# A three-stage fused kernel (retention, gated feed-forward, routed experts): a different order of work at the start of the expert stage and inside its phases

## The chip, the cores and the metric

The kernel runs on one core of a Trainium2 chip. The metric is the time of one execution on the device in microseconds (us), the median of several runs. A profile of one further execution comes with it. Engines: PE (TensorE), DVE (VectorE), ACT (ScalarE), POOL (GpSimd), and SP, which only issues DMAs here.

## The reference, cut to what matters

Three layers follow each other on 2304 tokens of 512 values.

1. Retention: `scores = q @ k.T / 8`, multiplied by a decay matrix per head, times `v` (4 batches, 8 heads, 576 positions, 64 values).
2. Feed-forward: `h = x @ w_in` (2048 columns), `g = h * tanh(softplus(h))`, `y = g @ w_out`.
3. Routed experts: eight experts with 288 places each. The pairs (token, expert) are taken in the order of falling logit; a token gets the first expert that still has a place. Then, for every expert,

```python
mask = assigned == e
h = np.maximum(x[mask] @ w1[e], 0.0)      # 512 -> 1024
out[mask] = h @ w2[e]                     # 1024 -> 512
```

## The kernel before, in words

Matrix products are made from two fp32r pieces per operand, hi and lo (`hi*hi + hi*lo + lo*hi`), so a logical product is three matmuls. Layers 1 and 2 take the first 517 us of the profile and are not touched. They leave the rows `y` in DRAM (`ydram`), the logits `L` in SBUF, and tiles for the search. All that follows is in `second_part`.

**Phases.** The experts are settled one after another: phase `ph` finds the expert that fills up next, its 288 tokens, and computes it. The search (`routing_fast`, a generator) has three levels: DVE compares every token's best logit with 66 thresholds (`reach`, L719, in two instructions, tokens 0 to 8 and 9 to 17 of a partition), PE counts (`cnt`, L1003, 18 small matmuls), DVE picks the interval. A tail of short DVE instructions settles the expert (`EINT`), updates `L` and prepares the next search. The compaction (L878 to L932) turns token positions into a list of row numbers: DVE writes three one-hot tiles `hot` (L900), PE sums them into `pi` (L907, three times six small matmuls), DVE makes the integers `ix`. The `gather` (L1239) then fetches the rows by three indirect DMAs of 96 rows that POOL issues; `transposes` turns them on PE and splits them (ACT hi, DVE lo).

**The expert.** `ffn(ph)` issues 192 matmuls of 288 columns, yielding after each: eight column blocks of `w1` (12 matmuls each; L1287, output `hp`), then four of `w2` (24 each; L1301, output `op`). After each `hp` group ACT writes hi and DVE lo (`htl`, L1278); a later group's bank waits for them.

**Weights.** An expert has eight tiles of 128x1024 (512 KB). `fetch` issues the load on SP into one of four buffers `wraw`; `split` lets ACT write the hi tile and POOL the lo tile (L841, L843). Tile `i` of the first four holds row block `i` of `w1`, so any column block needs all four; the second four hold two row blocks of `w2` each, and again any output block needs all four.

**The order** is written out while the program is built. A set of estimated clocks (`clk`) follows each engine; after every expert matmul the loop decides by them whether to issue a search step, a piece of the compaction (`fills`), a due lo part (`urgent`), a split, a gather or a transpose. A search step ends where the generator yields its DVE cost and a PE cost. `pieces(ph, n)` forces splits until `n` tiles of a phase are made, on DVE for every second one: eight at matmul 92, four of the next phase at a phase's end.

**The start of the stage.** No expert work exists yet, so search 0, its compaction, the first gather, the split of the first four weight tiles (ACT hi, DVE lo), the first level of search 1 and the transposes follow in a fixed order (L1363 to L1387). All small PSUM values of the search, and `pi`, lie in one bank, `dv`; wherever PE writes a bank that DVE reads, the framework orders the two.

Of the kernel before, what the change touches and what calls it, by code (L numbers as in the profile page):

```python
# [7 lines left out]
F32 = mybir.dt.float32  # L8
# [619 lines left out]
DG = 0.05  # L628
RM = (0, 0.1)
X = mybir.AxisListType.X  # L630

# [142 lines left out]
def second_part(ctx, tc, L, ydram, wx, cst, out, st, fast, L0=None):  # L774
# [30 lines left out]
    else:  # L805
        off, one18 = st.off, st.one18
    spacer = c2.tile([1, 1], F32, name="spacer")

    def rt(shape, name, dt=F32, bufs=2):
# [8 lines left out]

    def fetch():

        while len(fetched) < 4 and SRC.get("next", 0) // 8 in EINT:
            n = SRC.get("next", 0)
            ph, i = n // 8, n % 8
            if i == 0:
                r = nc.sync.value_load(EINT[ph], min_val=0, max_val=E - 1)
                SRC[ph] = wx[bass.ds(r, 1)].rearrange("o p f -> p (o f)")
            raw = wk.tile([P, 1024], F32, tag="wraw", name="wraw", bufs=4)
            if n == 4:

# [47 lines left out]
    def compaction(ph, slot):  # L877


        if fast:  # L880
            pi = pi_[ph % 2][:96].rearrange("p (k c) -> p k c", c=2)
            col, col1, at = col_[ph % 2], col1_[ph % 2], at_[ph % 2]
        else:
            pi = psum.tile([96, 3, 2], F32, tag="pi", name="pi")
            col = col1 = rt([P, NT], "col")
            at = rt([P, NT], "at", BF)
# [11 lines left out]
        def part(c0, ready, n=6):  # L898
            hot = rt([P, n, 96], "hot", BF, bufs=3)
            V.tensor_tensor(hot, bc(io[:, None, :], [P, n, 96]),  # L900
                            bc(at[:, c0:c0 + n, None], [P, n, 96]), op=ALU.is_equal)
            on_dve(0.75)
            ready[:] = [clk["dve"] + 0.15]
            yield
            clk["pe"] += 0.06 * n
            for c in range(n):
                nc.tensor.matmul(pi, hot[:, c, :], cv[:, c0 + c, :, :], start=(c0 + c == 0),  # L907
                                 stop=(c0 + c == NT - 1))
# [17 lines left out]
        fills.append((None, go(gens[1][1])))  # L926
        fills.append((gens[0][0], go(gens[0][1])))
        fills.append((None, go(gens[2][1])))
        fills.append((gens[1][0], go(gens[1][1])))
        fills.append((gens[2][0], go(gens[2][1])))  # L930
        fills.append((None, end))
        COMP.append(ph)  # L932

    def routing_fast():
# [29 lines left out]
        for ph in range(E):  # L964
            sel = rt([P, NT], "sel")
            rs = rt([P, 1], "rs", BF)
            if ph < E - 1:
# [7 lines left out]
                for lv in range(3):  # L975
                    end = lv == 2
                    if lv or ph:
                        ind = st.tile([P, NT, NW], "ind", BF)
                        st.reach(ind, tau, NW, 0, 9)
                        if not lv:  # L980
                            st.one_hot(0, NT)
                        st.reach(ind, tau, NW, 9, NT)
# [4 lines left out]
                    if end:  # L987
                        below = rt([P, 1], "below")
                        V.tensor_scalar(below, tau[:, 0:1], stp[:, 2:3], None, op0=ALU.subtract)
                    yield (F0[ph > 0], F1, F2)[lv], 0.65  # L990
                    if not (ph or lv):
# [40 lines left out]
                m0 = rt([P, NT], "m0n")  # L1032
                V.tensor_reduce(m0, L, axis=X, op=ALU.max)
                its = rt([P, NT], "its")
                V.tensor_tensor(its, m, m0, op=ALU.is_gt)
# [16 lines left out]
            EINT[ph] = ei[0:1, 0:1]  # L1052
            pend = (ph, sel, rs, dm)
            if ph < 2 or ph >= E - 2:
                yield 2.4, 0.06
                rest, pend = slots(*pend), None
                rest()
                yield 1.2, 0.0
# [178 lines left out]
    scat = []  # L1237

    def gather(ph):  # L1239
        xg = wk.tile([96, 3, DM], F32, tag="xg", name="xg")  # L1240
        for k in range(3):
            nc.gpsimd.indirect_dma_start(
                out=xg[:, k, :], out_offset=None, in_=ydram[:, :],
                in_offset=bass.IndirectOffsetOnAxis(ap=IDX[ph][:, k:k + 1], axis=0))
        XG[ph] = xg

# [22 lines left out]
    def ffn(ph):  # L1269
# [11 lines left out]
        for ft in range(F // P):  # L1281
            hp = psum.tile([P, CAP], F32, tag="fp", name="hp", bufs=3)
            s = slice(ft * P, (ft + 1) * P)
            k = 0
            for w, x in ((0, xh), (0, xl), (1, xh)):
                for kt in range(KT):
                    nc.tensor.matmul(hp, W[kt][w][:, s], x[:, kt, :], start=(k == 0), stop=(k == 11))  # L1287
                    k += 1
                    if k == 12:
                        nc.scalar.activation(hh[:, ft, :], hp, AF.Relu)  # L1290
                        urgent.append((clk["pe"] + (0.6 if ft < F // P - 1 else 0.0), lambda ft=ft, hp=hp: rest(ft, hp)))
                    yield
        ot = wk.tile([P, KT, CAP], F32, tag="ot", name="ot")
        OT[ph] = ot
        for dt in range(KT):
            op = psum.tile([P, CAP], F32, tag="fp", name="op", bufs=3)
            k = 0
            for w, h in ((0, hh), (1, hh), (0, hl)):
                for ft in range(F // P):
                    s = slice((ft % 2) * DM + dt * P, (ft % 2) * DM + (dt + 1) * P)  # L1300
                    nc.tensor.matmul(op, W[4 + ft // 2][w][:, s], h[:, ft, :], start=(k == 0),  # L1301
                                     stop=(k == 23))
# [45 lines left out]
    def step():  # L1348

        clk["pe"] = max(clk["pe"], clk["route"]) + nxt_pe[0]  # L1350
        try:
            cost, nxt_pe[0] = next(gen)
            on_dve(cost, clk["pe"] + 0.25)
            clk["route"] = clk["dve"] + 0.15
        except StopIteration:
            clk["route"] = 1e9

    def pieces(ph, n):
        while len(WSET.get(ph, ())) < n:
            fetch()  # L1360
            split(eng=V if len(WSET.get(ph, ())) % 2 else None)

    while 0 not in EINT:  # L1363
        step()
    fetch()
    los = [split(True) for i in range(4)]
# [17 lines left out]
    rush(True)  # L1384
    clk["pe"] = max(clk["pe"], clk["dve"])
    step()
    fetch()  # L1387
    for ph in range(E):
# [9 lines left out]
        for i, _ in enumerate(ffn(ph)):  # L1398
# [22 lines left out]
            if i in todo:  # L1421
# [5 lines left out]
        if nxt:  # L1427
# [12 lines left out]
            rush(True)  # L1440
            pieces(ph + 1, 4)
    while fills:
# [62 lines left out]
def host_layout(inputs):  # L1505
# [18 lines left out]
        "wx": c(np.concatenate([  # L1524
            inputs["moe2_w1"].reshape(E, KT, P, F).transpose(0, 2, 1, 3).reshape(E, P, KT * F),
            inputs["moe2_w2"].reshape(E, F // P, P, DM).transpose(0, 2, 1, 3).reshape(E, P, F // P * DM)], 2)),
    }
# [44 lines left out]
```

## Time and profile before

| | |
|---|---|
| three timed runs | 812.0, 812.57, 812.8 us; median 812.57 |
| profiled execution | 811.79 us, of which span 810.0 us |
| busy in the span | PE 758.4 us, POOL 475.3, DVE 543.7, ACT 435.7 |
| layers 1 and 2 | 0 to 517 us |
| start of the expert stage | 517 to 544 us |
| eight phases | 544 to 797 us |
| last stores | 797 to 810 us |

Times in the trace are counted from the start of the span. A matmul's end is modelled: a lone one shows 0.29 us where the next one starts 0.13 us later, so PE can look busy over a short loss; a loss is read from starts.

### The profile page before, as it was taken

The numbers are of one execution on the slowest core, as the hardware profiler recorded it, in microseconds if no ns is written. First come the engines' busy times: TensorE is split into PE (matmuls) and PEld (weight loads), VectorE is DVE, ScalarE is ACT, GpSimd is POOL, SyncE is SP. The second block draws the span as 40 slices with busy tenths as digits, with TensorE's granted clock in tenths as the row PEclk, the third lists the DMA queues.
The fourth block names the chain that finished last, engine by engine and source line by source line (L and its number), as shares of the span: only waits on it lengthen the run. The fifth ranks groups of instructions, "written<-read, shape, count | busy, mean of one in ns | idle before, by whom it ended". The sixth has DMA issues, their size and how long they took to land.

```text
span 810.0 us, 16286 instructions
## 1 busy us (share of the span) xinstructions
PE 758.4 (94%) x6163; PEld 699.2 (86%) x6163; DVE 543.7 (67%) x1262; ACT 435.7 (54%) x943; POOL 475.3 (59%) x539
## 2 busy tenths in 40 slices
PE   7799899999999999999999999849999999999993
PEld 6687777898988898999889899739999999999992
DVE  5999998645556898997989955676567473442110
ACT  4789998555535555555455555224545464464420
POOL 2643333645546676676767655215978996887711
PEclk9899999999999999999999999959999999999997
DMA  9556441010242211112100000063555764655301
GB/s 347 206 163 211 157 148 70 28 48 25 86 141 70 78 27 53 54 53 78 53 26 3 1 27 2 28 210 133 183 175 172 218 201 145 209 163 174 100 30 34
DMA packets 27321, 87.64 MB, mean 108 GB/s; under 512 B 4448, under 2 KB 5600, under 8 KB 27104
## 3 DMA queue, kind: packets, MB, share of 16 engines
q1 hardware_dynamic: 24160, 77.06, 29.1%
q0 software_dynamic: 3072, 9.44, 3.6%
q8 instruction: 50, 0.82, 0.4%
q14 instruction: 39, 0.32, 0.1%
HBM read 77.05 MB, written 9.44 MB: 107 GB/s over the span
## 4 chain that ended last, share of the span: by engine, by line
PE 69%; DVE 16%; issue 7%; DMA 2%; ACT 2%; POOL 2%; DVEq 0%; SPq 0%; POOLq 0%; ACTq 0%
PE ph L323 20%; PE hp L1287 9%; PE op L1301 9%; PE b_E L417 8%; PE b_F L417 8%; DVE rs L345 3%; DVE y L172 2%; DVE raw L167 2%; PE cnt L1003 2%; PE b_A L223 1%; DVE u L350 1%; DVE hot L900 1%; PE b_E L453 1%; PE b_D L252 1%; PE b_F L453 1%
## 5 line engine op out<-in xcount | busy, mean ns | idle before, releaser
L323 PE MATMUL ph<-xh,winh 128*128 128x256 f32 x576 | 165.1, 287 | 7.9 <-ACT d L332 4.8
L323 PE MATMUL ph<-xl,winh 128*128 128x256 f32 x576 | 161.4, 280 | 1.2 <-DVE xl L259 1.2
L323 PE MATMUL ph<-xh,winl 128*128 128x256 f32 x576 | 161.2, 280 | 0.0
L843 POOL TENSOR_TENSOR wxl<-wraw,wxh 128x1024 fp32r<-128x1024 f32 x60 | 142.3, 2397 | 23.9 <-ACT wxh L841 23.6
L323 PEld LDWEIGHTS ph<-xh,winh 128*128 128x128 f32 x576 | 108.7, 189 | 22.8 <-ACT d L332 9.1
L365 POOL TENSOR_TENSOR gl<-u,gh 128x256 fp32r<-128x256 f32 x114 | 88.4, 776 | 64.9 <-ACT gh L364 64.0
L332 ACT ACTIVATE d<-ph 128x256 f32<-128x256 f32 x144 | 55.0, 382 | 132.2 <-PE ph L323 120.0
L323 PEld LDWEIGHTS ph<-xh,winl 128*128 128x128 f32 x576 | 109.1, 189 | 4.1
L323 PEld LDWEIGHTS ph<-xl,winh 128*128 128x128 f32 x576 | 109.4, 190 | 1.7 <-DVE xl L259 1.7
L345 DVE RECIPROCAL u<-u 128x128 f32<-128x128 f32 x113 | 107.7, 953 | 3.9
L340 DVE TENSOR_TENSOR u<-d 128x128 f32<-128x128 f32 x113 | 52.1, 461 | 63.3 <-ACT d L334 58.5
L352 POOL TENSOR_TENSOR u<-d,u 128x128 f32<-128x128 f32 x112 | 51.9, 464 | 58.2 <-DVE u L345 58.2
L841 ACT ACTIVATE wxh<-wraw 128x1024 fp32r<-128x1024 f32 x64 | 67.4, 1053 | 17.8 <-DMA wraw<-in_wx_dram 17.7
L333 ACT ACTIVATE d<-d,half_b 128x256 f32<-128x256 f32 x144 | 73.5, 511 | 4.7
L353 POOL TENSOR_TENSOR u<-d,u 128x128 f32<-128x128 f32 x112 | 68.7, 613 | 8.8
L334 ACT ACTIVATE d<-d 128x256 f32<-128x256 f32 x144 | 60.2, 418 | 4.5
L364 ACT ACTIVATE gh<-u 128x256 fp32r<-128x256 f32 x144 | 58.0, 403 | 5.3 <-DVE u L358 4.1
L374 DVE SCALAR_TENSOR_TENSOR scr<-y,WG 128x512 bf16<-128x512 f32 x64 | 56.5, 882 | 0.4
L1278 DVE SCALAR_TENSOR_TENSOR htl<-hp,hth 128x288 fp32r<-128x288 f32 x64 | 28.4, 454 | 39.6 <-ACT hth L1290 39.0
L358 DVE SCALAR_TENSOR_TENSOR u<-u,ph 128x256 f32<-128x256 f32 x144 | 52.1, 362 | 0.0
L1290 ACT ACTIVATE hth<-hp 128x288 fp32r<-128x288 f32 x64 | 26.2, 409 | 47.4 <-PE hp L1287 46.9
L1287 PE MATMUL hp<-xth,wxh 128*128 128x288 f32 x256 | 49.4, 307 | 1.3 <-DVE htl L1278 1.2
(279 smaller groups left out, 1881.8 us busy)
## 6 DMA issues: line engine op xcount, KB each, us to landing
wraw<-in_wx_dram SPq DMA_DIRECT2D x64, 512.0 KB, 4.2
att<-in_att_dram SPq DMA_DIRECT2D x32, 512.0 KB, 5.0
raw<-in_wi_dram SPq DMA_DIRECT2D x16, 512.0 KB, 3.6
raw<-in_wo_dram SPq DMA_DIRECT2D x16, 512.0 KB, 3.4
ydram<-y SPq DMA_DIRECT2D x9, 512.0 KB, 2.8
WG<-in_wgb_dram SPq DMA_DIRECT2D x1, 2048.0 KB, 7.9
att<-in_att_ht_dram SPq DMA_DIRECT2D x4, 256.0 KB, 4.0
att<-in_att_hn_dram SPq DMA_DIRECT2D x4, 256.0 KB, 4.1
```

Of the source, the lines that this page charges most:

```text
L323: nc.tensor.matmul(ph, w[f][:, kt, :], x[:, kt, :], start=(k == 0), stop=(k == 11))
L333: nc.scalar.activation(df, df, AF.Square, bias=half_b, scale=-0.5)
L334: nc.scalar.activation(df, df, AF.Copy, bias=0.5, scale=0.5)
L345: nc.vector.reciprocal(r, r)
L353: eng.tensor_mul(u[:, 0, :], d[:, 1, :], r)
L364: nc.scalar.activation(gh, g, AF.Copy)
L365: eng.tensor_sub(gl, g, gh.bitcast(F32))
L417: nc.tensor.matmul(py[n][t], g[:, t * P:(t + 1) * P], w[f], start=(f == 0 and w is woh and g is gh), stop=(f == NF - 1 and g is gl))
L841: nc.scalar.activation(hi, raw, AF.Copy)
L843: rest = lambda eng: eng.tensor_sub(lo, raw, hi.bitcast(F32))
L1287: nc.tensor.matmul(hp, W[kt][w][:, s], x[:, kt, :], start=(k == 0), stop=(k == 11))
L1301: nc.tensor.matmul(op, W[4 + ft // 2][w][:, s], h[:, ft, :], start=(k == 0), stop=(k == 23))
```

## The change: what it does

- The one-hot sums `pi` of phase 0 get a bank of their own (a free buffer of `fp`). For later phases they stay in `dv`, but all three `hot` tiles are written first and the 18 sums follow in one run.
- Two weight tiles are loaded before the first gather instead of four. The third load waits for a POOL instruction behind the gathers. Of the first two tiles DVE makes one lo part, after the first level of search 1 has been issued, and POOL the other, after DVE's is done.
- A gather of row 0 into the first gather buffer stands at the head of the stage; nothing reads it.
- After the first gather DVE copies one value that POOL writes behind the gathers, ahead of the next `reach`.
- The search after the first steps yields between the two `reach` instructions, and in its tail, with other estimated costs; the second step of search 1 moves from ahead of the first expert matmul into the loop.
- The weights are laid out by columns: a tile of `w1` holds two whole column blocks, one of `w2` one output block, so one tile is needed per 24 matmuls. Forced splits come four matmuls ahead of each need (`DUE`), and only one tile is forced at a phase's end. In phase 0 the first column block uses its lo weights before the lo rows.

```diff
+DUE = {24 * k - 4: k + 1 for k in range(1, 8)}
...
-    def fetch():
-        while len(fetched) < 4 and SRC.get("next", 0) // 8 in EINT:
+    def fetch(most=4):
+        while len(fetched) < most and SRC.get("next", 0) // 8 in EINT:
...
-            if n == 4:
+            if n == 2:
                 nc.gpsimd.memset(raw[:, 0:1], 0.0)
...
-            pi = pi_[ph % 2][:96].rearrange("p (k c) -> p k c", c=2)
+            pi = pi_[ph % 2] if ph else psum.tile([P, CAP], F32, tag="fp", name="pi", bufs=3)
+            pi = pi[:96, :6].rearrange("p (k c) -> p k c", c=2)
...
-            ready[:] = [clk["dve"] + 0.15]
+            ready[:] = [clk["dve"] + (0.5 if ph else 0.15)]
...
+        if ph:
+            def products():
+                for t, g in gens:
+                    next(g, 0)
+            fills.append((None, go(gens[2][1])))
+            fills.append((gens[2][0], products))
...
+                    parts = ph > 1 or ph and lv
...
+                        if hold:
+                            hold.pop()()
                         st.reach(ind, tau, NW, 0, 9)
+                        if parts:
+                            yield 1.15, 0.0, 1
...
-                    yield (F0[ph > 0], F1, F2)[lv], 0.65
+                    yield ((1.1, 1.05, 1.0) if parts else (F0[ph > 0], F1, F2))[lv], 0.65
...
                 V.tensor_reduce(m0, L, axis=X, op=ALU.max)
+                if ph:
+                    yield 1.4, 0.1, 1
...
+            if 1 < ph < E - 2:
+                yield 1.2, 0.0, 1
             if ph < 2 or ph >= E - 2:
-                yield 2.4, 0.06
+                yield (1.2 if ph else 2.4), 0.06
...
+XG[0] = wk.tile([96, 3, DM], F32, tag="xg", name="xg")
+row_dma(0, 0, nought)
 while 0 not in EINT:
     step()
-fetch()
-los = [split(True) for i in range(4)]
+fetch(2)
+los = [split(True) for i in range(2)]
 while not fills:
     step()
 fill(True)
 gather(0)
-los[0](V)
-los[1](V)
-step()
-los[2](V)
-los[3](V)
+nc.gpsimd.memset(spacer, 0.0)
+fetch()
+hold.append(lambda: V.tensor_copy(after, spacer))
+step()
+los[0](V)
+nc.gpsimd.tensor_copy(spacer, WSET[0][0][1][0:1, 0:1].bitcast(F32))
+los[1](nc.gpsimd)
...
 rush(True)
-clk["pe"] = max(clk["pe"], clk["dve"])
-step()
-fetch()
+clk["dve"] = clk["pe"]
+clk["route"] = clk["pe"] + 0.1
...
-                clk["pool"] = max(clk["pool"], clk["pe"]) + 3.1
-                there = clk["pool"] + GD
+                clk["pool"] = max(clk["pool"], clk["pe"], clk["dve"] + 0.9) + 3.5
+                there = clk["pool"] + 2.3
...
-            if i == 92:
-                pieces(ph, 8)
+            if i in DUE:
+                pieces(ph, DUE[i])
...
-            pieces(ph + 1, 4)
+            pieces(ph + 1, 1)
```

The host lays `w1` and `w2` out accordingly, and `ffn` slices `W[ft // 2]` and `W[4 + dt]`.

## Rows read from the trace of the kernel before

**Rows 1.** Windows by stage: stretch, length, busy (instructions) by engine, PEclk, DMA share, GB/s

```profile
517.31:544.10 26.79, 11.80 (x136) 10.36 (x134) 20.41 (x64) 6.01 (x9) 4.06 (x5) 0.62 0.42 145
544.10:577.19 33.09, 33.04 (x301) 32.21 (x301) 21.73 (x70) 14.26 (x26) 20.37 (x11) 0.95 0.48 158
577.19:612.62 35.43, 33.66 (x335) 32.51 (x334) 23.95 (x88) 17.46 (x30) 30.05 (x20) 1.00 0.62 186
612.62:646.61 33.99, 32.93 (x313) 31.98 (x312) 20.90 (x72) 17.87 (x30) 29.98 (x20) 1.00 0.63 194
646.61:679.05 32.44, 31.89 (x296) 30.97 (x294) 17.28 (x58) 15.72 (x27) 26.96 (x21) 1.00 0.66 199
679.05:710.20 31.15, 30.90 (x277) 30.28 (x276) 14.15 (x54) 15.50 (x27) 24.73 (x18) 1.00 0.58 173
710.20:739.58 29.38, 29.23 (x238) 28.96 (x237) 10.60 (x42) 15.76 (x27) 24.66 (x18) 1.00 0.61 180
739.58:767.65 28.07, 28.07 (x219) 27.98 (x218) 5.96 (x15) 15.49 (x27) 22.45 (x16) 1.00 0.39 117
```

**Rows 2.** Timeline of the start: start, us, engine, line, operation, [idle before <-releaser]

```profile
532.55 0.56 PE L907 MATMUL dv<-cv,hot 128*96 128x6 bf16 x6 [3.17 <-DVE hot L900]
533.15 0.75 DVE L900 TENSOR_TENSOR hot<-c_io,dv 128x576 bf16<-128x576 bf16 x1 [0.66 <-PE dv L907]
533.96 1.05 PE L907 MATMUL dv<-cv,hot 128*96 128x6 bf16 x12 [0.84 <-DVE hot L900]
...
535.70 1.23 DVE L843 TENSOR_TENSOR wxl<-wraw,wxh 128x1024 fp32r<-128x1024 f32 x1
...
536.28 1.64 POOL L1242 DMA_INDIRECT xg<-ydram,ix  x1 [16.16 <-DVE dv L957]
...
538.22 1.10 POOL L1242 DMA_INDIRECT xg<-ydram,ix  x1 [0.30 <-issue]
...
538.87 0.78 DVE L719 TENSOR_TENSOR ind<-dv,g_G 128x594 bf16<-128x594 f32 x1
...
539.62 0.92 POOL L1242 DMA_INDIRECT xg<-ydram,ix  x1 [0.30 <-issue]
...
541.46 0.90 PE L1248 MATMUL tp<-c_ident,xg 96*128 96x96 f32 x4 [0.55 <-DMA xg<-ydram,ix]
...
542.16 1.18 PE L1003 MATMUL cnt<-oh,ind 128*66 128x8 bf16 x18
...
543.20 0.88 PE L1248 MATMUL tp<-c_ident,xg 96*128 96x96 f32 x4
...
544.10 1.51 PE L1287 MATMUL hp<-xth,wxh 128*128 128x288 f32 x4
```

**Rows 3.** Timeline of PE around a later compaction, and who waited for `hot`

```profile
593.54 0.64 PE L1287 MATMUL hp<-xth,wxl 128*128 128x288 f32 x3
594.53 0.39 PE L907 MATMUL dv<-cv,hot 128*96 128x6 bf16 x6 [0.34 <-DVE hot L900]
594.78 0.38 PE L1287 MATMUL hp<-xth,wxl 128*128 128x288 f32 x1
...
  PE dv L907: 5.5, 7
```

**Rows 4.** Timeline of phase 2 where an expert matmul waits for DVE

```profile
627.53 0.69 PE L1287 MATMUL hp<-xth,wxl 128*128 128x288 f32 x4
...
628.24 1.18 DVE L1278 SCALAR_TENSOR_TENSOR htl<-hp,hth 128x288 fp32r<-128x288 f32 x3
...
628.74 0.79 PE L1287 MATMUL hp<-xth,wxh 128*128 128x288 f32 x4 [0.51 <-DVE htl L1278]
```

**Rows 5.** Timeline of phase 1 where a transpose waits for the gather

```profile
602.92 0.30 PE L1248 MATMUL tp<-c_ident,xg 96*128 96x96 f32 x1 [0.78 <-DMA xg<-ydram,ix]
```

**Rows 6.** Groups of instructions: the weight split on POOL and ACT (mean ns behind busy us)

```profile
L843 POOL TENSOR_TENSOR wxl<-wraw,wxh 128x1024 fp32r<-128x1024 f32 x60 | 142.3, 2397 | 23.9 <-ACT wxh L841 23.6
L841 ACT ACTIVATE wxh<-wraw 128x1024 fp32r<-128x1024 f32 x64 | 67.4, 1053 | 17.8 <-DMA wraw<-in_wx_dram 17.7
```

More of the change, by code (lines that the diff above doesn't have):

```diff
@@ L807, in second_part @@
     spacer = c2.tile([1, 1], F32, name="spacer")
+    after = c2.tile([1, 1], F32, name="after")
+    nought = c2.tile([96, 1], I32, name="nought")
+    nc.gpsimd.memset(nought, 0)
+    hold = []
     def rt(shape, name, dt=F32, bufs=2):
@@ L926, in compaction @@
         fills.append((None, go(gens[1][1])))
[L927 to L930, printed above, removed]
+        if ph:
[4 more added lines that the diff above has]
+            fills.append((gens[2][0], products))
+        else:
+            fills.append((gens[0][0], go(gens[0][1])))
+            fills.append((None, go(gens[2][1])))
+            fills.append((gens[1][0], go(gens[1][1])))
+            fills.append((gens[2][0], go(gens[2][1])))
         fills.append((None, end))
@@ L1237, in second_part, with row_dma @@
     scat = []
+    def row_dma(ph, k, ix):
+        nc.gpsimd.indirect_dma_start(
+            out=XG[ph][:, k, :], out_offset=None, in_=ydram[:, :],
+            in_offset=bass.IndirectOffsetOnAxis(ap=ix, axis=0))
     def gather(ph):
-        xg = wk.tile([96, 3, DM], F32, tag="xg", name="xg")
+        if ph:
+            XG[ph] = wk.tile([96, 3, DM], F32, tag="xg", name="xg")
         for k in range(3):
[L1242 to L1245, printed above, removed]
+            row_dma(ph, k, IDX[ph][:, k:k + 1])
     def turn(tp, ph, k, kt):
@@ L1282, in ffn @@
             hp = psum.tile([P, CAP], F32, tag="fp", name="hp", bufs=3)
-            s = slice(ft * P, (ft + 1) * P)
             k = 0
-            for w, x in ((0, xh), (0, xl), (1, xh)):
+            for w, x in ((0, xh), (0, xl), (1, xh)) if ph or ft else ((0, xh), (1, xh), (0, xl)):
                 for kt in range(KT):
-                    nc.tensor.matmul(hp, W[kt][w][:, s], x[:, kt, :], start=(k == 0), stop=(k == 11))
+                    s = slice(kt * (F // 4) + (ft % 2) * P, kt * (F // 4) + (ft % 2 + 1) * P)
+                    nc.tensor.matmul(hp, W[ft // 2][w][:, s], x[:, kt, :], start=(k == 0), stop=(k == 11))
                     k += 1
@@ L1299, in ffn @@
                 for ft in range(F // P):
-                    s = slice((ft % 2) * DM + dt * P, (ft % 2) * DM + (dt + 1) * P)
-                    nc.tensor.matmul(op, W[4 + ft // 2][w][:, s], h[:, ft, :], start=(k == 0),
+                    s = slice(ft * P, (ft + 1) * P)
+                    nc.tensor.matmul(op, W[4 + dt][w][:, s], h[:, ft, :], start=(k == 0),
                                      stop=(k == 23))
@@ L1351, in step @@
         try:
-            cost, nxt_pe[0] = next(gen)
-            on_dve(cost, clk["pe"] + 0.25)
-            clk["route"] = clk["dve"] + 0.15
+            cost, nxt_pe[0], *more = next(gen)
+            on_dve(cost, clk["pe"] + (0.0 if more else 0.25))
+            clk["route"] = clk["dve"] + (-0.2 if more else 0.15)
         except StopIteration:
@@ L1524, in host_layout @@
         "wx": c(np.concatenate([
-            inputs["moe2_w1"].reshape(E, KT, P, F).transpose(0, 2, 1, 3).reshape(E, P, KT * F),
-            inputs["moe2_w2"].reshape(E, F // P, P, DM).transpose(0, 2, 1, 3).reshape(E, P, F // P * DM)], 2)),
+            inputs["moe2_w1"].reshape(E, KT, P, 4, F // 4).transpose(0, 2, 3, 1, 4).reshape(E, P, KT * F),
+            inputs["moe2_w2"].reshape(E, F // P, P, KT, P).transpose(0, 2, 3, 1, 4).reshape(E, P, F // P * DM)], 2)),
     }
```

## The prediction

> **What bounds the kernel now.** I read the windows first, stage by stage, because the change leaves layers 1 and 2 alone. From 544 us on PE bounds: phase 6, which has no search left, takes 28.07 us with PE busy in all of it, and its neighbours are longer by what PE does for the search and by what PE waits [rows 1]. Ahead of that lies the start, 517.31 to 544.10 us, where PE is busy for 11.80 of 26.79 us at a mean granted clock of 0.62; there a chain through DVE, POOL, DMA and PE decides [rows 1, 2]. Second came the timeline of that chain, third the places in the phases where PE waits.
>
> The phases hold less than they seem to. Length less PE busy is 1.77, 1.06, 0.55, 0.25 and 0.15 us in phases 1 to 5, 3.8 us in all [rows 1]. Since ends are modelled, each stall hides another 0.16 us or so; by starts I find 5.8 us in phases 0 to 5, of three kinds:
>
> - Compaction: 3.1 us in eight places. In the place shown three expert matmuls start at 593.54 and PE's next start is at 594.53: 0.99 less 3 times 0.13 and the 0.09 below is 0.51 us [rows 3]. The others are 0.21 to 0.51.
> - DVE bursts: two `reach` and a one-hot run without a break, the lo part `htl` comes after them, and an expert matmul waits for its bank: 628.74 less 627.53 is 1.21, less 4 times 0.13 is 0.69 us [rows 4]. With two more places (0.83 and 0.27) 1.8 us.
> - One transpose that stands in PE's queue before its gather has landed, idle for 0.78 and late by 0.94 us [rows 5].
>
> **The start, step by step.** Before, the third `hot` waits for the first six sums (0.66 idle) and the other twelve wait for it, since `pi` lies in the bank that `hot`'s input lies in; the sums end at 533.96 + 1.05 = 535.01 [rows 2]. With a bank of its own `hot` 3 follows `hot` 2 at once, at 532.5, ends at 533.25, and the last six sums (0.56) at 533.86: 1.15 us earlier.
>
> Gathers: the first issue takes 1.64 us and the second 1.10, the third 0.92 [rows 2]. The first two lie beside DVE's lo splits of 1.23 us. The splits move behind the search step, so three issues of 0.92, 0.30 apart, start at 535.13, 536.35 and 537.57 and end at 538.49, against 540.54. By starts, a gather's transposes can begin 541.46 - 538.22 = 3.24 us after its issue, so the rows are there at 540.8 instead of 542.9.
>
> The copy behind the gathers is an added wait: behind it on DVE stand `reach`, one-hot, `reach` (538.87 to 540.54, 1.67 us), the lo split and the count's reader; PE's count waits for the `reach`, and the third transposes queue behind the count. POOL's memset (0.09) and the two hand-overs put the copy's end at about 538.7, so `reach` ends at 540.4 against 540.54 before: the wait takes back what DVE had won, but no more. The count, which before had to queue behind transposes that ended at 541.46 + 0.90 = 542.36, can now run at 540.5. From there to the first expert matmul it was 544.10 - 542.36 = 1.74 us [rows 2]; the new first matmul starts at 542.25, **1.85 us earlier**. Bounds: were the copy free, the third gather would decide (540.8 + 0.9 = 541.7, 2.4 us earlier); were the gathers no faster and the bank worth nothing, the copy would put `reach` at 540.7 and the first matmul 0.2 us later than now.
>
> The clock: half speed (1.2 of 2.4 GHz) lasts from the start into phase 0, whose mean is 0.95: 0.05 / 0.5 of 33.09 us is 3.3 us at the lower level [rows 1]. I let its end move along with the start; if it stays where it is, half of the 1.85 us is lost, 0.9.
>
> What could be late next? The lo part of tile 0 comes from DVE after `reach`, 540.4 + 1.23 = 541.7, ahead of its use four half-speed matmuls after 542.25. Tile 1 is POOL's until 544.2, needed after 24 matmuls, about 548; tiles 2 and 3 are loaded from 538.6 on, 5 to 7 us before a use at 551 and later. POOL takes over three lo parts, 3 x 2.40 = 7.2 us [rows 6]; it is busy for 20.37 of 33.09 us in phase 0 [rows 1], so I cost it at nothing. The unread gather is issued while POOL is idle anyway (16.16 us ahead of the first real one, [rows 2]) and costs nothing.
>
> What does it bring? It could only remove the slow first issue, 1.64 - 0.92 = 0.7 us, if that was code arriving. But the first issue overlaps DVE's splits for 1.27 us and is 0.72 late, the second for 0.31 and is 0.18 late, the same 0.57 of the overlap: I read both as contention, and the splits' move has already paid for them. The Trainium skill (GPSIMD Engine Reference, 2.1 Instruction dispatch) says that the first call of a freshly loaded GpSimd kernel pays about 6 us for its code; by that the unread gather would be worth about 6 us more. No run here shows it: the whole excess is 0.7 us. The same page (1. Specifications) has GpSimd's SBUF interfaces contending with DVE instructions that have two SBUF inputs, which fits the splits; the sum is the same by either reading of the 0.7 us, as the change removes both causes.
>
> **The phases, step by step.** Later compactions keep `pi` in DVE's bank, but write all `hot` first and sum once. That removes most of the 3.1 us; I take 2.5, since one wait per compaction can remain. It also saves returns: the first expert matmul after a small group lasts 0.38 us instead of 0.29 [rows 3, 4], and two groups fewer in six compactions are 12 x 0.09 = 1.1; I take 0.8. Smaller pieces let `htl` in between: of the 1.8 us I take 1.2. The later estimate for landed gathers spares the late transpose: 0.5 of 0.94, as the matmuls behind may become short. No instruction is added by the pieces, but about five step ends per search, each of which may put a PE instruction ahead of its data; bounds 0 and, at 0.25 us (half the usual loss) for one in two ends of six searches, 3.7 us. I take 0.9.
>
> The weights by columns move nothing on PE and relax what is due: one tile per 24 x 0.13 = 3.1 us against 2.40 us on POOL [rows 6].
>
> Sum: -1.85 - 2.5 - 0.8 - 1.2 - 0.5 + 0.9 = **-5.95 us** on the profiled execution (span 810.0, 1.8 around it: 811.8), so 805.8. The median of the runs shown is 0.8 above that execution, and I forecast 806.6 us for the runs.
>
> **The rivals.**
>
> *The bank wait only moves.* With 18 sums in one run DVE is shut out of the bank for 18 x 0.045 = 0.8 us, and the sums wait for any `reach` (0.78) already issued that reads the search's values there. The Trainium skill (PSUM — Partial Sum Buffer, PSUM bank collisions raise a hardware error) has any two engines on one bank kept apart, reads too; the rows agree, `hot` and sums alternate [rows 2, 3]. One such wait in each of six compactions is 6 x 0.78 = 4.7 us: the phases bring nothing, the start stays, 812.6 - 1.85 = 810.7. For it: the bank is still shared. Against: the readiness estimate rises by 0.35 us, and PE has other matmuls until then.
>
> *Late weight tiles, slower than before.* A split forced four matmuls ahead has 0.5 us, but needs 1.05 + 2.40 = 3.45 on ACT and POOL [rows 6]: 2.9 us of PE each. It begins where POOL falls more than a tile behind; the third late tile eats the gain. POOL is busy for 30.05 of 35.43 us in phase 1 [rows 1], and before, the first four tiles were forced only at a phase's end. One in each of phases 1 to 6 is 17.4 us: 806.6 + 17.4 = 824. Against it: all 60 lo parts of before ran on POOL, so no forced DVE split was ever needed, though four tiles were due at once.
>
> *The copy does not do what it should.* The gathers stay slow, or the clock does not move along: the start brings about nothing, the phases -4.1: 808.5.
>
> **How the numbers follow.** Forecast 0.60 (804 to 809, by the bounds of the start and the phases' terms); the moved bank wait 0.21 (809.5 to 812); the empty start 0.10; late tiles 0.09. The range 803.5 to 811.3 leaves out late tiles, the upper third of the moved wait and a little below. This kernel's runs tell 0.2%, 1.6 us, from nothing: faster means under 810.9. The forecast, the empty start and a third of the moved wait give 0.77; the rest of the moved wait 0.13 the same; late tiles and a little of the moved wait 0.10 slower.
>
> **What would show it.** Start: `pi` read at 533.9, three issues of 0.92 us, the first expert matmul at 542.3. Phases: one run of 18 sums per compaction without a wait, no `htl` wait ahead of an expert matmul, phase 1 down by 2 us or more, phase 6 still 28.1. Wrong would be: a first issue of 1.6 us beside an idle DVE, sums waiting for `reach`, or an expert matmul that waits for a lo tile.

## The result and the profile after

The changed kernel takes 801.51 us (median of four runs, 800.3 to 802.5), the kernel before, beside it, 812.58 (812.0 to 812.8): a ratio of 0.9875, interval 0.9859 to 0.9892. The forecast was 806.6 us with 803.5 as the low end: the direction is right, the gain is nearly twice as large (11.1 us where 6.0 were expected), and the time lies below the range.

The profiled execution took 802.28 us (span 800.5) against 811.79. These 9.5 us are, by stage: the start ends 2.45 us earlier, phases 0 to 5 are 7.37 us shorter in sum, phases 6 and 7 0.49, and the tail behind the last matmul is 0.80 longer (13.30 to 14.10; in m_unread, which differs from the changed kernel at the start alone, it is 13.34). The medians differ by 1.6 us more: this profiled run of the changed kernel lies 0.8 above its median, that of the kernel before 0.8 below.

The windows by stage of the changed kernel, columns as in [rows 1], here with the last phase and the tail behind it:

```profile
517.22:541.65 24.43, 12.64 (x135) 10.82 (x133) 16.77 (x62) 3.90 (x7) 4.78 (x10) 0.57 0.38 123
541.65:574.62 32.97, 32.34 (x301) 31.57 (x302) 22.27 (x71) 15.33 (x27) 25.65 (x13) 0.96 0.56 179
574.62:607.49 32.87, 32.87 (x336) 32.39 (x334) 21.11 (x80) 17.51 (x29) 28.29 (x20) 1.00 0.64 194
607.49:639.58 32.09, 32.09 (x314) 31.68 (x313) 22.23 (x77) 17.65 (x29) 28.00 (x19) 1.00 0.61 186
639.58:670.74 31.16, 31.16 (x295) 30.80 (x294) 18.33 (x61) 16.55 (x28) 29.82 (x20) 1.00 0.69 211
670.74:701.04 30.30, 30.30 (x277) 30.03 (x276) 13.97 (x54) 15.72 (x27) 27.34 (x21) 1.00 0.67 207
701.04:729.78 28.74, 28.74 (x239) 28.64 (x238) 10.72 (x42) 15.49 (x27) 24.06 (x17) 1.00 0.59 179
729.78:757.62 27.84, 27.84 (x219) 27.75 (x218) 5.96 (x15) 15.72 (x27) 23.26 (x17) 1.00 0.44 133
757.62:786.40 28.78, 28.28 (x218) 27.77 (x216) 3.73 (x9) 7.20 (x17) 3.02 (x6) 1.00 0.07 21
```

In phases 1 to 5 PE is now busy for the whole length; in [rows 1] 1.77, 1.06, 0.55, 0.25 and 0.15 us were left over. Phase 0 hardly moved (33.09 to 32.97). Phase 6 has neither search nor compaction and is nevertheless 0.2 us shorter.

The timeline of the start, columns as in [rows 2]:

```profile
524.88 1.12 POOL L1264 DMA_INDIRECT xg<-ydram,nought  x1 [4.81 <-issue]
...
531.32 2.07 DVE L906 TENSOR_TENSOR hot<-c_io,dv 128x576 bf16<-128x576 bf16 x3
532.12 1.97 PE L913 MATMUL pi<-cv,hot 128*96 128x6 bf16 x18 [2.51 <-DVE hot L906]
...
534.32 0.16 DVE L920 SCALAR_TENSOR_TENSOR ix<-pi,pis 96x3 int32<-96x3 f32 x1
534.75 0.92 POOL L1264 DMA_INDIRECT xg<-ydram,ix  x1 [8.76 <-DVE dv L972]
...
535.98 0.92 POOL L1264 DMA_INDIRECT xg<-ydram,ix  x1 [0.30 <-issue]
...
537.21 0.92 POOL L1264 DMA_INDIRECT xg<-ydram,ix  x1 [0.30 <-issue]
...
538.13 0.09 POOL L1400 MEMSET spacer<- 1x1 f32 x1
...
538.25 0.14 DVE L1402 COPY after<-spacer 1x1 f32<-1x1 f32 x1 [3.07 <-POOL spacer L1400]
538.32 0.75 DVE L720 TENSOR_TENSOR ind<-dv,g_G 128x594 bf16<-128x594 f32 x1
...
541.65 0.61 PE L1314 MATMUL hp<-xth,wxh 128*128 128x288 f32 x1
```

Here the reader sees three one-hots without a break, the first 18 sums in one run, three equal issues, and the copy 0.03 us behind the end of POOL's memset. From the first one-hot to the first expert matmul it is 10.33 us, before 13.01: 2.68 less, where 1.85 were forecast. (The kernels below that keep the old start unchanged take 12.79 to 12.99; against them it is 2.46 to 2.66.) The issue begins 0.27 us behind the end of `ix` (534.32 + 0.16). Before, that gap was 0.89, from 535.39 to the issue at 536.28 [rows 2]; the timeline of before has `ix` at

```profile
535.23 0.16 DVE L914 SCALAR_TENSOR_TENSOR ix<-dv,pis 96x3 int32<-96x3 f32 x1
```

A later compaction, to be held against [rows 3]: 18 sums in one run, and the expert matmul behind them follows without a gap:

```profile
590.44 0.69 PE L1328 MATMUL op<-hth,wxh 128*128 128x288 f32 x4
...
590.97 0.93 PE L913 MATMUL dv<-cv,hot 128*96 128x6 bf16 x18
...
591.76 0.77 PE L1328 MATMUL op<-hth,wxh 128*128 128x288 f32 x4
```

What PE still waits for in the phases (us, times, longest; before, the list had `hot` with 1.5 in five, `htl` with 1.2 in two, the gather with 0.8 and the same wait for `ot`, the output of the last phase):

```profile
PE tp L1275 <- DVE xtl L1292: 0.6, 1, 0.6
PE tpo L1342 <- ACT ot L1332: 0.5, 1, 0.5
```

### The profile page after: what moved, and what is told of

It reads as the page before. It is cut to its first block, busy times and chain, and to the rows that moved or that the text cites. A ratio compares the mean times of both kernels' runs of the same rounds, so it can differ in the third digit from the quotient of the medians.

```text
span 800.5 us, 16293 instructions
## 1 busy us (share of the span) xinstructions
PE 754.1 (94%) x6163; PEld 697.0 (87%) x6163; DVE 540.1 (67%) x1260; ACT 435.3 (54%) x943; POOL 483.3 (60%) x546
## 4 chain that ended last, share of the span: by engine, by line
PE 73%; DVE 12%; issue 6%; ACT 3%; POOL 3%; DMA 3%; SPq 0%; DVEq 0%; POOLq 0%; ACTq 0%
PE ph L323 20%; PE hp L1314 10%; PE op L1328 10%; PE b_E L417 8%; PE b_F L417 8%; DVE rs L345 3%; DVE y L172 2%; PE cnt L1023 2%; DVE raw L167 2%; POOL wxl L848 2%; DMA raw<-in_wi_dram 1%; PE b_A L223 1%; DVE u L350 1%; PE b_E L453 1%; PE b_D L252 1%
## 5 line engine op out<-in xcount | busy, mean ns | idle before, releaser
L848 POOL TENSOR_TENSOR wxl<-wraw,wxh 128x1024 fp32r<-128x1024 f32 x63 | 149.4, 2397 | 6.0 <-ACT wxh L846 5.5
L1314 PE MATMUL hp<-xth,wxl 128*128 128x288 f32 x256 | 48.0, 302 | 0.0
```

What stands on the lines that cost most here:

```text
L848: rest = lambda eng: eng.tensor_sub(lo, raw, hi.bitcast(F32))
L1314: nc.tensor.matmul(hp, W[ft // 2][w][:, s], x[:, kt, :], start=(k == 0), stop=(k == 11))
```

## The experiments

Phase lengths below run from the first `hp` of one phase to that of the next. Ratios are to the kernel before on the same chip. Numbers in brackets behind a ratio are its 95% interval. `p_` kernels are built up from before, `m_` take a part out of the changed kernel, `s_` put one part alone into before, `v_` try to go further.

### What shortens the phases

**p_order**: the sums of later compactions in one run, nothing else.

```diff
-            ready[:] = [clk["dve"] + 0.15]
+            ready[:] = [clk["dve"] + (0.5 if ph else 0.15)]
...
+            fills.append((None, go(gens[2][1])))
+            fills.append((gens[2][0], products))
```

> The kernel before with one edit: for phases after the first, the three one-hot tiles are written first and their 18 sums follow in one run, in the shared bank. Theory A (the terms of the prediction were right and only cut too far): the whole 3.1 us of waits and 1.1 us of returns go, about 4.0 us, 808.6. Theory B (the orders of the phases only work together): the waits move to other places, under 1.5 us, 811 to 812.6. By the moved bank wait: no change or slower.

Measured: 811.47 us, 1.0001 (0.999 to 1.0013). The waits for `hot` are gone, and others have come, most of them for `xtl`, the lo part of the transposed rows (us, times, longest):

```profile
PE tp L1257 <- DVE xtl L1274: 1.7, 2, 1.0
PE hp L1296 <- DVE xtl L1274: 1.7, 2, 1.1
PE op L1310 <- POOL wxl L843: 0.8, 1, 0.8
```

The timeline of p_order at the end of phase 1:

```profile
608.56 0.77 DVE L719 TENSOR_TENSOR ind<-dv,g_G 128x594 bf16<-128x594 f32 x1
...
609.24 0.81 DVE L1274 TENSOR_TENSOR xtl<-tp,xth 128x288 fp32r<-128x288 f32 x2
...
609.84 0.44 PE L1257 MATMUL tp<-c_ident,xg 96*128 96x96 f32 x3 [1.04 <-DVE xtl L1274]
```

A `reach` stands ahead of the split of the transposed rows, and the last transposes wait for their bank. Counted in expert matmuls the search comes later here than before: the two `reach` of this step start when 168 and 175 of the phase's 192 have begun, before when 153 and 160 had. Why DVE is later is not shown. The saving is given back in these waits.

**p_pieces**: the small search pieces with their estimated costs, nothing else.

```diff
+                        if parts:
+                            yield 1.15, 0.0, 1
...
+                if ph:
+                    yield 1.4, 0.1, 1
...
```

> The kernel before with one edit: the search yields between its two threshold comparisons and in its tail, with the changed kernel's cost estimates. Theory A: the 1.8 us that expert matmuls wait behind VectorE's bursts go and nothing is added, 810.8. Theory B: more step ends put PE instructions ahead of their data, so no gain or a loss, 812 to 814.

Measured: 813.21 us, 1.0019 (1.0008 to 1.003): slightly slower. The `htl` waits are gone, but `hot` waits grow to 2.6 us in seven places, one of them in the timeline:

```profile
619.66 0.74 DVE L900 TENSOR_TENSOR hot<-c_io,dv 128x576 bf16<-128x576 bf16 x1
...
620.46 0.39 PE L907 MATMUL dv<-cv,hot 128*96 128x6 bf16 x6 [0.56 <-DVE hot L900]
```

**p_columns**: weights by columns, nothing else (slices and host layout).

```diff
-                    nc.tensor.matmul(hp, W[kt][w][:, s], x[:, kt, :], start=(k == 0), stop=(k == 11))
+                    nc.tensor.matmul(hp, W[ft // 2][w][:, s], x[:, kt, :], start=(k == 0), stop=(k == 11))
...
```

> The kernel before with one edit: the weights laid out by columns, with the forced splits as before. The prediction said that this moves nothing on PE: 812.6, with phase 6 at 28.07 us. Rival: a matmul starts about 1 ns earlier after the one ahead when successive weights come from one tile, as phases 6 and 7 of the changed kernel suggest (27.84 and 28.78 us against 28.07 and 29.05): 8 x 0.22 = 1.8 us, 810.8, phase 6 at 27.85.

Measured: 811.08 us, 1.0002 (0.9991 to 1.0013). Nothing in before waits for a lo tile, so there is nothing to relax.

**p_phases**: all that the change does inside the phases, with the old start.

> The kernel before with all edits of the phases and none of the start: one run of sums, search pieces, weights by columns with their forced splits, the later gather estimate. If the two halves of the change add up, the phases bring the 7.8 us that their lengths lost in the profile: 804.8, and the rest, 2.4 us or more, is the start's. If the phases need the new start, they bring clearly less, 807 to 810.

Measured: 805.26 us, 0.992 (0.9903 to 0.9936). The windows of its phases 0 to 5:

```profile
544.04:577.26 33.22, 32.74 (x301) 32.01 (x301) 22.28 (x71) 13.43 (x25) 18.76 (x10) 0.95 0.43 145
577.26:610.14 32.88, 32.88 (x336) 32.41 (x335) 21.05 (x80) 17.51 (x29) 28.32 (x20) 1.00 0.65 192
610.14:642.26 32.12, 32.12 (x315) 31.71 (x314) 22.27 (x78) 17.61 (x29) 28.03 (x19) 1.00 0.63 188
642.26:673.48 31.22, 31.22 (x296) 30.88 (x294) 18.35 (x61) 16.52 (x28) 29.81 (x20) 1.00 0.69 209
673.48:703.83 30.35, 30.35 (x276) 30.08 (x275) 13.98 (x54) 15.72 (x27) 27.35 (x21) 1.00 0.68 206
703.83:732.56 28.73, 28.73 (x239) 28.64 (x237) 10.64 (x42) 15.49 (x27) 24.05 (x17) 1.00 0.60 180
```

They sum to 188.52 us against 195.50, 6.98 less. The three edits above, each of which brings nothing or a loss alone, bring 6.2 us of the median together with the later gather estimate.

**p_pair** (one run of sums and small pieces) and **p_pair_cols** (these, the weights by columns, and splits forced one tile at a time).

> The kernel before with two edits together: the 18 sums in one run and the small search pieces; each alone brought nothing. Theory C: each edit removes its own wait and uncovers the other's (one run alone left waits for lo parts behind two comparisons, small pieces alone left waits for the one-hot tiles), so that only the pair shortens the phases: 806 to 807.5, no PE wait for hot, htl or xtl over 0.6 us. Rival D: what shortens the phases is the weights by columns with splits due one by one, and the pair brings under 2 us: 810 to 812.

> The pair and the weights by columns with their forced splits, without the later gather estimate. Theory C: as the pair, 806 to 807.5, or up to 1 us less where the pair has a matmul waiting for a weight tile. Rival D: here first the phases shorten, to 805 to 806, while the pair alone stays over 810. A PE wait for the gather of phase 1 (0.8 us before) shows whether the gather estimate is needed too.

Measured: p_pair 808.19 us, 0.9955 (0.9939 to 0.9972), between what the two theories gave; p_pair_cols 805.8, 0.9928 (0.9914 to 0.9943). In p_pair phases 2 to 5 take 32.58, 31.22, 30.35 and 28.73 us, 4.1 less than before in sum and, but for phase 2, the lengths of the changed kernel within 0.1: neither `hot` nor `htl` holds them up. But phases 0 and 1 take 34.49 and 35.26: among other waits PE reaches a lo tile before POOL has made it, and POOL had itself waited 0.95 us for ACT's hi tile. The timeline of p_pair:

```profile
580.03 2.37 POOL L843 TENSOR_TENSOR wxl<-wraw,wxh 128x1024 fp32r<-128x1024 f32 x1 [0.95 <-ACT wxh L841]
...
582.45 0.40 PE L1303 MATMUL hp<-xth,wxl 128*128 128x288 f32 x1 [1.00 <-POOL wxl L843]
```

In p_pair_cols this wait and its like (0.5 us) are gone, and the two phases take 33.37 and 33.82. The later gather estimate, which is all that p_phases has beyond p_pair_cols, spares the transposes' waits for the gather (1.3 us in two places) and brings phases 1 and 2 to 32.88 and 32.12.

**p_pair_lay**, **r_lay** (one kernel, on two chips) and **r_cols** (p_pair_cols again, beside r_lay): is it the layout or the forced splits? The first two have the layout with the splits forced as before, eight tiles at matmul 92 and four of the next phase at a phase's end; the diff is against the changed kernel.

```diff
-DUE = {24 * k - 4: k + 1 for k in range(1, 8)}
...
-            if i in DUE:
-                pieces(ph, DUE[i])
+            if i == 92:
+                pieces(ph, 8)
...
-            pieces(ph + 1, 1)
+            pieces(ph + 1, 4)
```

> The pair (one run of sums, small search pieces) with the weights by columns, but the splits forced as before: eight tiles at matmul 92, four at a phase's end. If the layout alone takes away the pair's waits for weight tiles (1.0 us in phase 1, 0.5 in phase 0), phases 0 and 1 are 33.4 and 33.8 us as with the single forced splits, 805.8. If forcing them one by one does it, they are 34.5 and 35.3, 808.2.

> The same kernel as p_pair_lay (sums in one run, small pieces, weights by columns, splits forced as before), now on one chip with r_cols, so that the two are compared without a chip between them. Theory 1 (the one-by-one forced splits are what the columns are worth): 0.9950 to 0.9960, 2 us behind r_cols, with PE waits of 3 us or more that r_cols does not have. Theory 2 (the layout alone is enough, and the waits for DVE's result of a count in p_pair_lay belonged to that chip): within 0.0008 of r_cols.

> The same kernel as p_pair_cols (sums in one run, small pieces, weights by columns, splits forced one tile at a time), beside r_lay on one chip: by both theories 0.9920 to 0.9935 of the kernel before, phases 0 and 1 at 33.4 and 33.8 us.

Measured: p_pair_lay 810.91 us, 0.9957 (0.9944 to 0.9971), as if the layout brought nothing. But it ran on another chip than p_pair and p_pair_cols, one where before took 814.16, and its phase 2 took 36.27 us with a wait that the others don't have:

```profile
625.00 0.16 PE L1025 MATMUL dg<-cl,c_ones 66*128 66x1 bf16 x1 [2.01 <-DVE full L1019]
```

A stop of DVE like that (1.6 us in phase 2) stands in s_splits on the same chip and in s_alloc and s_addr on another where before took 814.71; what stops DVE there is not shown. Side by side on one chip r_lay took 805.19 us, 0.9922 (0.9905 to 0.9938), and r_cols 806.2, 0.9935 (0.992 to 0.995); their phases agree within 0.03 us. The windows of r_lay's phases 0 and 1:

```profile
543.18:576.22 33.04, 32.47 (x301) 31.77 (x302) 22.22 (x71) 13.36 (x25) 19.21 (x10) 0.96 0.45 154
576.22:609.98 33.76, 33.06 (x336) 32.33 (x334) 21.96 (x83) 18.56 (x31) 29.12 (x20) 1.00 0.64 185
```

So it is the layout; forcing the splits singly adds nothing that can be measured. What the layout is worth is read on one chip from p_pair to p_pair_cols: phases 0 and 1 are 2.56 us shorter, some 0.4 of them by an earlier rise of PE's clock (3.6 us behind the first expert matmul instead of 4.4).

### What shortens the start

**m_unread**: the changed kernel without the unread gather.

```diff
-row_dma(0, 0, nought)
```

> The changed kernel without the unread gather. If GpSimd's first gather is slow by itself, its first issue is back at 1.6 us or begins 0.9 us behind ix instead of 0.27, and the first expert matmul comes 0.5 to 1 us later. If the slow issue was contention with VectorE's splits alone, as the prediction said, the issue stays at 0.92 us and the time moves by under 0.2 us.

Measured: 801.74 us, 0.9875 (0.9857 to 0.9894), as with it. The first real gather's issue now takes the 1.12 us that the unread one took, so a first indirect DMA costs 0.20 us more than a later one here, and the unread gather moves that off the path. From the first one-hot to the first expert matmul it is 10.60 us without it, 0.27 more, too little to be seen in the time.

The Trainium skill (GPSIMD Engine Reference, 2.1 Instruction dispatch) has about 6 us for a first call of a freshly loaded kernel; nothing of that size shows in this trace, where the first issue took 0.20 us more than the later ones.

**m_hold**: the changed kernel without DVE's copy behind the gathers.

```diff
-    hold.append(lambda: V.tensor_copy(after, spacer))
```

> The changed kernel without VectorE's copy behind the gathers. The comparisons then begin some 3 us earlier, and the lo split runs beside the second and third gather. Contention theory: those issues take 1.1 to 1.6 us instead of 0.92, so the third gather lands later, but the count no longer queues ahead of its transposes; the first expert matmul comes 0 to 0.5 us earlier. If the copy earns its place, it comes later.

Measured: 802.4 us, 0.9896 (0.9877 to 0.9916). DVE gets to its lo split 0.40 us ahead of the third gather's issue. The timeline of m_hold:

```profile
535.49 1.22 DVE L848 TENSOR_TENSOR wxl<-wraw,wxh 128x1024 fp32r<-128x1024 f32 x1
...
535.89 1.61 POOL L1264 DMA_INDIRECT xg<-ydram,ix  x1 [0.30 <-issue]
```

The issue begins while the split still has 0.82 us to go (535.49 + 1.22 - 535.89), and takes 1.61 us instead of the 0.92 that it has in the changed kernel. The first expert matmul comes 10.83 us after the first one-hot, 0.5 later than with the copy. The time alone would not tell m_hold, or the next kernel, from the changed kernel: the intervals overlap.

**m_bank0**: the changed kernel with the first compaction's sums back in DVE's bank.

> The changed kernel with the first compaction's sums back in the shared bank. The prediction gave the own bank 1.15 us: the third one-hot tile waits for the first six sums again, and from the first one-hot tile to the first expert matmul 10.33 us become 11.5. If another wait hides it, 10.3 to 10.8. Second question: phases 6 and 7 take 27.85 and 28.78 us in the changed kernel, 28.07 and 29.05 without the new start; if the free buffer that the sums take from the expert's three banks does that, they are back at 28.07 and 29.05.

Measured: 802.99 us, 0.9899 (0.9882 to 0.9916); from the first one-hot to the first expert matmul 11.57 us, 1.24 more. The waits of [rows 2] are back with the same figures:

```profile
532.67 0.75 DVE L905 TENSOR_TENSOR hot<-c_io,dv 128x576 bf16<-128x576 bf16 x1 [0.66 <-PE dv L912]
...
533.48 1.05 PE L912 MATMUL dv<-cv,hot 128*96 128x6 bf16 x12 [0.84 <-DVE hot L905]
```

**s_splits**: before, with DVE's first two lo splits moved behind the first step of search 1.

```diff
     gather(0)
+    step()
     los[0](V)
     los[1](V)
-    step()
```

> The kernel before with one move: VectorE's first two lo splits come after the first level of search 1 instead of ahead of it. If the splits are what delays the first gather, its issue begins 0.28 us behind ix instead of 0.89 and takes 1.1 instead of 1.64 us, though nothing else of the new start is there; later issues meet the moved splits. From the first one-hot tile to the first expert matmul 12.0 to 12.6 us instead of 13.01. If the gap belongs to something else in the new start, it stays at 0.89.

Measured: 814.47 us, 1.0 (0.9991 to 1.0009). The issues take 1.12, 0.92 and 0.92 us: without a split already under way the first falls from 1.64 to the 1.12 of a first one. The gap behind `ix` stays 0.90. The start takes 12.47 us from the first one-hot, 0.54 less than in before and 0.32 to 0.52 less than in the other kernels with the old start, too little to be seen in the time.

**s_alloc**: before, with the tile of the first gather allocated at the head of the stage.

```diff
-        xg = wk.tile([96, 3, DM], F32, tag="xg", name="xg")
+        xg = XG[0] if ph == 0 else wk.tile([96, 3, DM], F32, tag="xg", name="xg")
...
+    XG[0] = wk.tile([96, 3, DM], F32, tag="xg", name="xg")
     while 0 not in EINT:
         step()
```

> The kernel before with one edit: the tile of the first gather is allocated at the head of the expert stage, ahead of the first search, so the gather's first issue no longer has to wait for PE's reads of that place (it waits for the loads and for DVE's row numbers alone). Theory (a wait that stands in an instruction of its own ahead of the indirect DMA costs 0.6 us between the row numbers and the issue): the long wait on POOL's queue ends on the DMA itself, the first issue begins 0.27 to 0.29 us behind ix instead of 0.89, all three gathers and the first expert matmul are 0.3 to 0.6 us earlier, 0.9993 to 1.000 of before. Rival (the 0.89 belongs to the old order of the start, DVE's splits beside the issue): 0.89 stays and nothing moves.

Measured: 813.57 us, 0.9988 (0.9978 to 0.9997). The issue begins 0.29 us behind `ix`. The gather's instructions at the start, in before, with duration of shortest, median and longest in ns, and first and last start:

```profile
L1242 POOLq EVENT_SEMAPHORE  x3: 17/43/11369, 519.8 to 524.1; - x3
```

and in s_alloc:

```profile
L1242 POOLq EVENT_SEMAPHORE  x2: 43/43/43, 523.1 to 523.2; - x2
L1242 POOL DMA_INDIRECT xg<-ydram,ix x2: 1121/1442/1762, 535.0 to 536.4; - x2
```

In before the wait for `ix` is an instruction of its own on POOL's queue (11.37 us long, until 535.43), because the gather also has to wait for PE's last reads of the buffer's place (the DMA itself waits there for one of PE's semaphores, in s_alloc for none of them); the DMA behind it begins 0.85 us after that. Where the tile is taken early that second wait is gone, the DMA itself waits for `ix`, and 0.6 us are saved there; the first expert matmul comes 12.53 us after the first one-hot, 0.48 less than in before and 0.26 less than in s_addr (12.79), which has the old start and ran on the same chip. It is less than 0.6 because the second issue now meets a split, as the next lines show. The changed kernel takes the tile early for its unread gather, m_unread takes it as early, and both have 0.27 or 0.28.

The same kernel shows when an issue beside a split is slow. The timeline of s_alloc:

```profile
535.01 1.12 POOL L1242 DMA_INDIRECT xg<-ydram,ix  x1 [15.77 <-DVE dv L954]
...
535.03 2.37 DVE L843 TENSOR_TENSOR wxl<-wraw,wxh 128x1024 fp32r<-128x1024 f32 x2
...
536.43 1.76 POOL L1242 DMA_INDIRECT xg<-ydram,ix  x1 [0.30 <-issue]
```

The first issue begins 0.02 us ahead of the splits, lies beside them throughout and takes the 1.12 us of any first one. The second begins with 0.97 us of a split to go and takes 0.84 more than 0.92. In m_hold 0.82 us to go cost 0.69; in before 0.30 to go cost the second issue 0.18 [rows 2]. In s_splits an issue that begins 0.12 us ahead of one split's end, with another split right behind, takes 0.92. So the issue waits for the end of the split that is already running, less 0.12 or 0.13 us; a split that begins after it costs nothing, nor does a `reach` (the changed kernel's unread issue begins with 0.72 us of one to go and takes 1.12). All issues at the start of the 20 kernels traced fit this.

### Addresses

**p_addr**: p_phases with the two small tiles that the changed kernel adds, written once by POOL and not used. **s_addr**: before with the same two tiles.

```diff
+    after = c2.tile([1, 1], F32, name="after")
+    nought = c2.tile([96, 1], I32, name="nought")
...
```

> The kernel before with all edits of the phases, as run before at 803.3 us of span, and two small tiles that only take up SBUF, as the new start's two do (GpSimd sets them to zero, nothing reads them). If the addresses of all later tiles make phases 6 and 7 shorter by 0.2 us each, they come at 27.85 and 28.78 us here; otherwise 28.07 and 29.05, and the time is that of the run without the tiles, 805.3.

> The kernel before with two small SBUF tiles that nothing reads (the names that the changed kernel adds, each written once), so that all later tiles move by some bytes. Theory (the last two phases are shorter in the changed kernel because of the tiles' addresses): phases 6 and 7 take 27.9 and 28.8 us instead of 28.07 and 29.05, and the whole 0.4 to 2 us less (phases that wait gain less): ratio 0.998 to 0.9995. Rival (the addresses count only together with the weights laid out by columns): 28.07 and 29.05, ratio 1.000.

Measured: p_addr 803.59 us, 0.9907 (0.9891 to 0.9923); s_addr 813.92, 0.9991 (0.9982 to 1.0001). Neither time is clear of noise against the kernel without the tiles; the phases are. The windows of phases 6 and 7 in s_addr; before had 28.07 [rows 1] and 29.05:

```profile
741.91:769.82 27.91, 27.91 (x220) 27.82 (x218) 5.96 (x15) 15.37 (x27) 22.42 (x16) 1.00 0.39 116
769.82:798.64 28.82, 28.32 (x218) 27.81 (x216) 3.73 (x9) 7.19 (x17) 3.00 (x6) 1.00 0.07 21
```

Two tiles that nothing reads shorten both phases by 0.2 us, in both kernels: the later tiles' addresses matter. The weights by columns do not do it (phase 6 of p_columns takes 28.07 us), nor does the bank of the first sums (27.85 in m_bank0). In phase 6, 87 distances between `hp` starts are under 150 ns; 17 of them are 140 ns in before and 5 in the changed kernel, and their mean falls from 133.0 to 131.0. What it is in the addresses is open.

### Two attempts to go further

**v_tp** issues no search step in phase 0 once the transposes have begun, against the 0.6 us wait for `xtl`; **v_both** also moves the copy from ahead of the `reach` to behind it, ahead of the lo split.

> The changed kernel with one condition: in phase 0 no search step is issued once the transposes have begun. Their lo parts then have no comparison ahead of them on VectorE, and the 1.0 us that PE loses there should go: phase 0 32.0 instead of 32.98 us, 800.5. If the later search makes the gather of phase 1 late, phase 1 gets longer by as much: no change.

> As the run before this one, and the copy behind the gathers is moved from ahead of the comparisons to ahead of the lo split. The third issue then stays at 0.92 us (1.61 beside the split without the copy) and the count is off the way of the third transposes: from the first one-hot tile to the first expert matmul 9.5 to 9.9 us instead of 10.33. If PE's clock then rises no earlier, half of that is lost in phase 0. 799.8 to 800.5.

Measured: 802.15 us, 0.9892 (0.9876 to 0.9908), and 802.79, 0.9899 (0.9883 to 0.9914). Phase 0 of v_tp falls to 32.42 us, but phase 1 rises to 33.32 and phase 3 to 32.0: the search that is left out of one phase is late in the next. In v_both the start takes 10.53 us where 9.5 to 9.9 were expected: PE still has the count between the second and the third transposes. No version beat the changed kernel. The order of the loads, the lo part that POOL makes and the lo weights used first in phase 0 were not tried by themselves; what they are worth is not shown.

## Why the prediction missed

**The step that failed** is the sum over the phases: -2.5 - 0.8 - 1.2 - 0.5 + 0.9 = -4.1 us where p_phases measured -6.98. It failed in three places.

- Each term was taken at less than its full size, for what might remain, and 0.9 us was added for new waits at step ends. The full terms (3.1 + 1.8 + 0.94 us of waits, 1.1 of returns) are 6.94, close to what was measured. Of new waits one of 0.6 us is left in phase 0.
- The terms were treated as independent. p_order and p_pieces show that each merely moves the wait to another place (1.0001 and 1.0019), and that the pair frees phases 2 to 5.
- The weights by columns were costed at nothing. That holds beside the old phases (p_columns), but not once these are short: behind the pair (0.9955) the kernels with the columns came to 0.9922, 0.9928 and 0.9935, 1.6 to 2.7 us less; a fourth, p_pair_lay, came to 0.9957 on the chip with the stop of DVE. The rival had looked for late lo tiles in the changed kernel; they come without the columns, in p_order, p_pieces and p_pair (0.8, 0.5 and 1.5 us of waits).

**The start** was forecast at -1.85 us and measured at -2.68, beyond the 2.4 that I gave as a bound. Right were the bank (1.15, m_bank0 1.24), three issues of 0.92, that the slow issues come from DVE's splits (m_hold, s_splits), and the copy as a wait that costs little. The size per overlap that I gave for the splits (0.57) was a chance agreement: 0.20 of the first issue's 0.72 us is its being first, and the rest is the wait for the running split (s_alloc). What the sum lacked is the wait in front of the first gather: 0.6 us of the 0.8 (s_alloc). The unread gather, costed at 0, brought its early tile and 0.27 us of its own (m_unread). The row for the wait, the 0.89 between `ix` and the issue, was in the timeline, and I took it for a fixed hand-over.

**Phase 6 "still 28.1"** was wrong by 0.2 us, the addresses; with phase 7 0.5 us, 0.4 of which the tiles alone bring in s_addr.

**Right** were: phase 1 down by 2 us or more (2.57), sums in one run without a wait, no `htl` wait, no late lo tile. The moved bank wait and the late weight tiles did not come. POOL is busy for 28.29 of 32.87 us in phase 1 and keeps ahead of PE.

**The clock** scatters, and I could not forecast it. Full speed comes, after the first expert matmul, 3.6 us later in before, 2.9 in the changed kernel, 5.3 in m_hold and 5.8 in v_both. That the end of half speed moves along with the start, as I had let it, came true by more than that: 0.7 us, which is 0.35 us of phase 0. The windows from the first expert matmul to full speed, in the changed kernel and in m_hold (the third column from the end is the granted clock, 0.50 of 2.4 GHz):

```profile
541.65:544.57 2.92, 2.92 (x12) 2.80 (x13) 2.88 (x7) 1.79 (x4) 2.92 (x2) 0.50 0.84 324
```

```profile
540.84:546.13 5.29, 5.29 (x22) 5.17 (x23) 3.84 (x9) 3.15 (x6) 2.71 (x2) 0.50 0.76 285
```

2.4 us more at half speed are 1.2 us of work lost: phase 0 takes 34.0 us in m_hold and 32.97 here. In part, then, the differences of the `m_` and `v_` kernels are this; r_lay and p_pair differ by it too (phase 0's mean clock 0.96 and 0.94).

## What to carry to other kernels

Where several small waits share one engine's time, taking out one moves the wait to the next place; they are worth their sum only together, so cost them jointly, at full size, and look for what each freed engine will run into. A gap between a result and the instruction that uses it is to be explained before it is taken as fixed: here a buffer allocated late put a second wait in front of a gather. Before an edit is said to bring nothing, ask whether that still holds when the others have worked, and compare variants on one chip.

## What was not expected of the hardware

- An indirect DMA's issue on POOL (0.92 us alone) waits for the end of a lo split that DVE has under way when it begins (1.61 with 0.82 to go, 1.76 with 0.97), and is not slowed by one that begins later (1.12 for a first one).
- A wait that stands in an instruction of its own ahead of an indirect DMA made the hand-over 0.89 us; a wait on the DMA itself 0.27 to 0.29.
- Moving tiles by some bytes changed a phase of 192 expert matmuls by 0.2 us.
- Two of the chips used were 3 us slower for the kernel before (814.2 and 814.7 against 810.9 to 812.6 on the others).
